# The first attention from tile 14 on: q and k come in as 32 by 32 blocks and VectorE transposes them, in place of TensorE

## The chip, the cores and the metric

One Trainium2 chip, of which the kernel uses one core. The metric is the device time of one execution in microseconds (us), the median of several executions; lower is better.

## The reference

Three layers follow one another, all in fp32. B = 8 sequences of S = 576 tokens, 8 heads of 64.

```python
# 1. attention inside chunks of 64 tokens (the "first attention")
scores = q_c @ k_c.T / sqrt(64)            # per batch, head, chunk: 64 x 64
attn = exp(scores - max); attn /= sum + 1e-9
x = (attn @ v_c)                           # heads side by side: B, S, 512
# 2. a mixing layer: each token with the one before it
xk = mu_k * x + (1 - mu_k) * x_prev;  xr = mu_r * x + (1 - mu_r) * x_prev
k = relu(xk @ w_k)                         # 512 -> 1024
v = (k * k) @ w_v                          # 1024 -> 512
r = sigmoid(xr @ w_r)                      # 512 -> 512
x = r * v
# 3. four experts, each a causal attention of one head of 64, the best two of four weighted
```

## The kernel before

`attn_mix` computes layers 1 and 2 together, `experts` layer 3 behind it. Nothing of `experts` is changed.

The 4608 tokens are cut in 36 tiles of 128 tokens, that is two chunks of 64, for the first attention, and in 12 units of 384 tokens for the mixing layer. For a tile the attention has these steps:

- `load_qk(t)` (L100): SP issues the loads of q and k of a tile. The buffers `ldq` and `ldk` are two deep, so the load of tile t + 2 is issued by `s_T(t)` when tile t has been read.
- `s_T(t)` (L132): `to_sbuf` turns q and then k by four TensorE transposes each (L127, into the PSUM bank `Tps`) and copies the result to SBUF by ScalarE (L129, `qT` and `kT`, two deep).
- `s_S(j)` (L142) takes a pair of tiles, 2j and 2j + 1: 64 matmuls of 64 x 64 on quarters of the TensorE array give the scores (`Sps`, L154). Then the softmax: VectorE takes the maximum (`m<-Sps`, L159) and subtracts it (`P<-Sps,m`, L160), ScalarE takes the exponential (L163), VectorE the sum (`m<-P`, L165) and its reciprocal (L167), GpSimd multiplies (L168).
- `s_PT(t)` turns the weights by four TensorE transposes (`Tps<-ident,P`), `s_PV(j)` (L172) multiplies by v (64 matmuls, L184) and ScalarE copies to `XT`. `load_v` (L107) loads v, which has four DMAs a tile.

The mixing layer of unit u has, in groups of 12 matmuls that each fill one of three PSUM buffers `mps`: 4 groups `mix_r` (emptied by ScalarE, L257), 8 groups `mix_k` and 4 double groups `mix_v`. A group of `mix_k` is emptied by ScalarE (L267, relu) and then VectorE (L270, `r<-mps,r`, which reads the PSUM buffer too and so sets it free); `kh` (ScalarE, L273) and `kl` (GpSimd, L274) are what `mix_v` reads. `mix_v` is emptied by VectorE (`x2o`, L289). The shifted inputs are made by GpSimd (`xa`, L228), VectorE (`xa`, L242; `xlr` and `xlk`, L244) and ScalarE (L243).

The steps of the attention are put between the groups of the mixing layer by a credit that is counted up with each group; the attention runs up to four units ahead of the mixing. The order on each engine is then fixed by a scheduler at build time, and each engine runs its list in order: an instruction that waits holds all that stand behind it on its engine. SP likewise issues its DMAs in the order of its list. The call `S` of pair j and `PV` of pair j - 1 stand together.

Of the kernel before, what the change touches and what calls it, by code (L numbers as in the profile page):

```python
# [8 lines left out]
F32 = mybir.dt.float32  # L9
# [10 lines left out]

CH = 64
UNIT = 384
CFG = dict(ps=(2, 3, 1, 2), P=5, sm=3, load=5, lag=(3, 4), out=(5, 1), qk1=(1, 1), qk0=(9, 1.1), v=(10, 0.9), order=((3, 0), (2, 0), (0, 0), (4, 0), (1, 0), (3, 1), (2, 1), (0, 1), (1, 1)), after=1, conv='v', clo='v', chi='g', x2hi='g', x2lo='v', ylo='g', yhi='v', xt='aa', r2='av', klo='vg', amul='vg', nearly=2, x2b=1, yb=4, qb=4, direct=((0, 1), (1, 1), (1, 1)), tailAV=4, kp=2, yt=1, yf=2, zb=1, om=(3, 2, 1, 0, 4), hp=1000, x2d=2, early=(2, 1), dact=3, rate0=0.43, rate=0.45, sh=(10, 12, 2), sh2=(11, 1, -1), pro='cccqqaacavvcaaaaacaacaaaascc', alag=2, seq=0, end=2, outL=(11, 2), outE=2, kcp='aa', dsc='v', ldb=2, vb=2, cn=512, stb=2, xb=4, pa=5, tb=2, first_j=7)
SEG = 192


# [7 lines left out]
def eng(nc, c):  # L34
    return nc.vector if c == "v" else nc.gpsimd
# [6 lines left out]
def copy(nc, c, out, in_):  # L42
    if c == "a":
        nc.scalar.activation(out=out, in_=in_, func=ACTF.Copy)
    else:
        eng(nc, c).tensor_copy(out, in_)
# [15 lines left out]
def attn_mix(tc, at, x2T, q, k, v, mu_k, mu_r, w_k, w_v, w_r, ident, attended_all, mixed_k):  # L62

    nc = tc.nc
    B, H, S, D = q.shape
    HP = H // 2
# [10 lines left out]
    with ExitStack() as ctx:  # L77
        wts = ctx.enter_context(tc.tile_pool(name="wts", bufs=1))
        mx = ctx.enter_context(tc.tile_pool(name="mx", bufs=1))
        ps = ctx.enter_context(tc.tile_pool(name="psM", bufs=1, space=PSUM))  # L80

        pa_open = ExitStack()
        pa = pa_open.enter_context(tc.tile_pool(name="psA", bufs=1, space=PSUM, side="right"))
# [9 lines left out]
        qkv = {}  # L93

        def runs(t):
            b, s = divmod(t * 128, S)
            return [(0, b, s, 128)] if s + 128 <= S else [(0, b, s, CH), (CH, b + 1, 0, CH)]

        def load_qk(t):
            for src, nm in ((q, "q"), (k, "k")):  # L100
                x = at.tile([128, H * D], F32, tag="ld" + nm, bufs=CFG["ldb"], name="ld" + nm)
                for p, b, s, n in runs(t):
                    nc.sync.dma_start(out=x[p:p + n].rearrange("p (h d) -> p h d", h=H),
                                      in_=src[b, :, s:s + n, :].rearrange("h p d -> p h d"))
                qkv[nm, t] = x

        def load_v(t):  # L107
            x = at.tile([128, 2, HP, D], F32, tag="ldv", bufs=CFG["vb"], name="ldv")
            for c in range(2):
                b, s = divmod(t * 128 + c * CH, S)  # L110
                for e in range(2):
                    r = e ^ c
                    nc.sync.dma_start(out=x[r * 64:(r + 1) * 64, c],
                                      in_=v[b, e::2, s:s + CH, :].rearrange("g p d -> p g d"))
            qkv["v", t] = x

        qT, kT, PP, PT, XT = {}, {}, {}, {}, {}
        nT = NU * TPU

        def bank(nm):  # L120
            return pa.tile([128, HP, 128], F32, tag="A", bufs=CFG["pa"], name=nm)

        def to_sbuf(src, nm):

            p = bank("Tps")
            for g in range(HP):
                nc.tensor.transpose(p[:, g], src[:, g * 128:(g + 1) * 128], ident)  # L127
            o = at.tile([128, HP, 128], F32, tag=nm, bufs=CFG["tb"], name=nm)
            nc.scalar.activation(out=o, in_=p, func=ACTF.Copy)  # L129
            return o  # L130

        def s_T(t):  # L132
            qT[t] = to_sbuf(qkv.pop(("q", t)), "qT")
            kT[t] = to_sbuf(qkv.pop(("k", t)), "kT")
            if t + CFG["ldb"] < nT:
                load_qk(t + CFG["ldb"])

# [6 lines left out]
        def s_S(j):  # L144
            banks = [bank("Sps").rearrange("p g (i k) -> p i g k", i=2) for _ in range(2)]
            for i in range(2):
                a, b = qT.pop(2 * j + i), kT.pop(2 * j + i)
                for g in range(HP):
                    for c in range(2):
                        for o in range(2):  # L150
                            e = o ^ c
                            r, cc = slice(e * 64, e * 64 + 64), slice(c * CH, (c + 1) * CH)
                            with tc.high_priority(1000) if j < CFG["first_j"] else nullcontext():
                                nc.tensor.matmul(out=banks[o][cc, i, g], lhsT=a[r, g, cc], rhs=b[r, g, cc],  # L154
                                                 start=True, stop=True)
            m = at.tile([128, 2, 2, HP], F32, tag="m", name="m")
            e = at.tile([128, 2, HP, 2, CH], F32, tag="P", name="P")
            for o, p in enumerate(banks):
                nc.vector.tensor_reduce(m[:, o], p, axis=AXX, op=ALU.max)  # L159
                nc.vector.tensor_tensor(e[:, :, :, o], p, m[:, o].unsqueeze(3).to_broadcast([128, 2, HP, CH]),  # L160
                                        op=ALU.subtract)
            ef = e.rearrange("p i g o k -> p (i g o) k")
            nc.scalar.activation(out=ef, in_=ef, func=ACTF.Exp, scale=scale)  # L163
            z = m.rearrange("p o i g -> p (o i g)")
            nc.vector.tensor_reduce(z, ef, axis=AXX, op=ALU.add)  # L165
            nc.vector.tensor_scalar(z, z, 1e-9, None, op0=ALU.add)
            nc.vector.reciprocal(z, z)  # L167
            eng(nc, CFG["amul"][j >= CFG["first_j"]]).tensor_tensor(  # L168
                ef, ef, z.unsqueeze(2).to_broadcast([128, 2 * H, CH]), op=ALU.mult)
            for i in range(2):  # L170
                PP[2 * j + i] = e[:, i]

        def s_PV(j):
            banks = [bank("PVps").rearrange("p g (i k) -> p i g k", i=2) for _ in range(2)]
            for i in range(2):
                t = 2 * j + i
                a, vt = PT.pop(t), qkv.pop(("v", t))
                for g in range(HP):
                    for c in range(2):
                        for o in range(2):  # L180
                            e = o ^ c
                            r, cc = slice(o * 64, o * 64 + 64), slice(c * CH, (c + 1) * CH)
                            with tc.high_priority(1000) if j < CFG["first_j"] else nullcontext():
                                nc.tensor.matmul(out=banks[c][e * 64:e * 64 + 64, i, g], lhsT=vt[r, c, g],  # L184
                                                 rhs=a[r, g, cc], start=True, stop=True)
            for c, p in enumerate(banks):

                done = 0
                while done < 2:
                    (u, k), n = divmod(4 * j + c + 2 * done, CH_U), 1  # L190
                    if u not in XT:
                        XT[u] = wkr.tile([128, HP, NSEG, SEG + 1], F32, tag="XT", bufs=CFG["xb"], name="XT")
                    sg, o = divmod(k, CPS)
                    if done == 0 and o + 2 < CPS:
                        n = 2
                    dst = XT[u][:, :, sg, 1:].rearrange("p g (w q) -> p w g q", q=CH)[:, o:o + 2 * n - 1:2]
                    copy(nc, CFG["xt"][u >= CFG["nearly"]], dst, p[:, done:done + n])
                    done += n
            for i in range(2):
                if 2 * j + i + CFG["vb"] < nT:  # L200
                    load_v(2 * j + i + CFG["vb"])
# [137 lines left out]
        for j in range(nT // 2 + 1):  # L339
            two = (2 * j, 2 * j + 1)  # L340
            attn += [(t // TPU, s_T, t) for t in two if t < nT]
            attn += [((t - 2) // TPU, s_PT, t - 2) for t in two if t > 1]
            attn.append(((2 * j - 1) // TPU if j else 0, s_SPV, j))
            attn += [(t // TPU, s_prev, t // TPU) for t in (2 * j - 2, 2 * j - 1) if t > 0 and t % TPU == TPU - 1]
# [32 lines left out]
        for c in CFG["pro"]:  # L377
            if c == "a":
                attend(2)
            elif c == "c":  # L380
                convert(1)
            elif c in loads:
                (load_qk if c == "q" else load_v)(next(loads[c]))
            else:
                attended(0)
                first_shift()

        credit = 0.0
        for u in range(NU):
# [6 lines left out]
            for i, (f, *args) in enumerate(items):  # L396
# [10 lines left out]
                if u + 1 < NU:  # L407
                    both = u + 1 <= CFG["sh2"][2]
                    for ws, at0 in (((1, 0), CFG["sh2"][0]),) if both else (((1,), CFG["sh"][0]), ((0,), CFG["sh"][1])):
                        g, r = divmod(i - at0, CFG["sh2" if both else "sh"][1 if both else 2])  # L410
# [508 lines left out]
```

## Time and profile before

| | |
|---|---|
| median of 3 runs (lowest to highest) | 1025.69 us (1022.12 to 1026.83) |
| the profiled execution | 1027.89 us |
| its span, from the first to the last instruction | 1026.1 us |
| granted TensorE clock over the span | 0.977 of full speed |
| busy over the span | PE 95%, PEld 91%, DVE 65%, ACT 56%, POOL 39% |
| from 183 to 510 us, where q and k of tiles 14 to 35 are turned | PE 324.8 of 327.0 us busy |

PE is TensorE's matmuls, PEld its weight loads, DVE VectorE, ACT ScalarE, POOL GpSimd, SP SyncE (SPq its DMA issues). The attention of all tiles ends at about 546 us; the experts take the rest. Busy shares are means over stages with different limits, so a change is judged in the stretch in which it stands.

### The profile page before, as it was taken

Reading aid. Unit: us, or ns where it says so; the run is one execution under the profiler, and the core shown is the slowest. Engines: PE = TensorE matmul, PEld = TensorE weight load, DVE = VectorE, ACT = ScalarE, POOL = GpSimd, SP = SyncE. Lnnn points to the kernel's source line nnn. Section 1 sums busy time; section 2 is a strip of 40 time slices with the busy share of each in tenths; the row PEclk is TensorE's granted clock in tenths of the full one; section 3 lists DMA queues with packets and bytes.
Section 4 is the critical chain, followed back from the end, with each engine's and each line's share of the span. In section 5 each row is a group of like instructions: output and inputs, shape, how many; then the busy total and the mean of one; then the engine's idle time right before and its main releaser. Section 6 shows DMA issues by size and latency. Waiting matters only on the chain.

```text
span 1026.1 us, 21849 instructions
## 1 busy us (share of the span) xinstructions
PE 972.5 (95%) x8214; PEld 934.0 (91%) x8214; DVE 664.5 (65%) x1646; ACT 570.0 (56%) x1315; POOL 395.6 (39%) x519
## 2 busy tenths in 40 slices
PE   3679899999999999999999999999999999999997
PEld 2569899998999999999999999989899999999986
DVE  5899935446544755565556541477776967787896
ACT  2478664545354636454635324266766757686675
POOL 5343312535453645364545443721341332133101
PEclk8588999999999999999999999999999999999999
DMA  8684432251324242425031211863545446262512
GB/s 220 176 210 134 113 84 73 52 124 43 98 48 124 63 104 48 114 45 126 22 83 39 76 47 37 190 160 86 172 96 160 136 117 183 68 178 69 171 42 95
DMA packets 170081, 108.39 MB, mean 106 GB/s; under 512 B 134024, under 2 KB 146424, under 8 KB 169976
## 3 DMA queue, kind: packets, MB, share of 16 engines
q1 hardware_dynamic: 139704, 67.14, 26.2%
q0 software_dynamic: 30272, 39.86, 14.3%
q8 instruction: 65, 1.06, 0.4%
q14 instruction: 40, 0.33, 0.1%
HBM read 66.01 MB, written 28.38 MB: 92 GB/s over the span
## 4 chain that ended last, share of the span: by engine, by line
PE 74%; DVE 12%; ACT 5%; DMA 4%; issue 2%; POOL 1%; SPq 1%; DVEq 0%; ACTq 0%; POOLq 0%
PE mps L57 14%; PE mps L59 14%; PE mps L58 14%; PE pj L57 6%; PE pj L59 5%; PE pj L58 5%; PE Sps L622 4%; PE Tps L127 3%; PE Tps L682 3%; PE AVps L715 2%; PE AVps L711 2%; PE Sps L154 2%; DVE PTl L689 1%; PE PVps L184 1%; DVE sm L624 1%
## 5 line engine op out<-in xcount | busy, mean ns | idle before, releaser
L57 PE MATMUL mps<-xhk,wkh 128*128 128x384 f32 x384 | 132.7, 347 | 2.0 <-DVE r L270 2.0
L58 PE MATMUL mps<-xlk,wkh 128*128 128x384 f32 x384 | 129.6, 338 | 0.0
L59 PE MATMUL mps<-xhk,wkl 128*128 128x384 f32 x384 | 129.4, 337 | 0.0
L57 PE MATMUL mps<-kh,wvh 128*128 128x384 f32 x384 | 129.1, 340 | 0.0
L58 PE MATMUL mps<-kl,wvh 128*128 128x384 f32 x384 | 127.7, 335 | 0.1
L59 PE MATMUL mps<-kh,wvl 128*128 128x384 f32 x384 | 126.9, 335 | 0.9 <-DVE wvl L325 0.9
L274 POOL TENSOR_TENSOR kl<-r,kh 128x384 fp32r<-128x384 f32 x80 | 86.1, 1080 | 79.7 <-ACT kh L273 79.5
L270 DVE TENSOR_TENSOR r<-mps,r 128x384 f32<-128x384 f32 x80 | 44.3, 554 | 99.8 <-ACT r L267 99.6
L634 ACT ACTIVATE P<-sm,nm 128x512 f32<-128x512 f32 (+3 forms) x144 | 83.9, 584 | 24.1 <-DVE nm L624 19.8
L228 POOL TENSOR_TENSOR xa<-XT 128x384 f32<-128x384 f32 x72 | 68.2, 955 | 62.3 <-DVE xlr L244 36.8
L624 DVE CUSTOM_DVE_ANT_0 sm<-Sps,mask 128x256 f32<-128x256 f32 (+4 forms) x160 | 74.2, 477 | 21.9 <-PE Sps L622 20.8
L731 POOL TENSOR_TENSOR Yf<-Yf,zb 128x576 f32<-128x576 f32 x14 | 20.0, 1430 | 153.5 <-DVE Yf L726 153.3
L57 PEld LDWEIGHTS mps<-xhk,wkh 128*128 128x128 f32 x384 | 72.9, 190 | 3.0 <-DVE r L270 2.5
L689 DVE TENSOR_TENSOR PTl<-Tps,PTh 128x512 fp32r<-128x512 f32 (+2 forms) x144 | 70.6, 504 | 7.0 <-ACT PTh L688 5.6
L242 DVE SCALAR_TENSOR_TENSOR xa<-xa,mu,XT 128x384 f32<-128x384 f32 x72 | 63.7, 900 | 15.0 <-POOL xa L228 14.9
L59 PEld LDWEIGHTS mps<-kh,wvl 128*128 128x128 f32 x384 | 71.8, 188 | 1.2 <-DVE wvl L325 1.2
L58 PEld LDWEIGHTS mps<-xlk,wkh 128*128 128x128 f32 x384 | 72.7, 189 | 0.1
L59 PEld LDWEIGHTS mps<-xhk,wkl 128*128 128x128 f32 x384 | 72.6, 189 | 0.0
L58 PEld LDWEIGHTS mps<-kl,wvh 128*128 128x128 f32 x384 | 72.1, 188 | 0.4 <-POOL kl L274 0.4
L57 PEld LDWEIGHTS mps<-kh,wvh 128*128 128x128 f32 x384 | 72.0, 188 | 0.4
L273 ACT ACTIVATE kh<-r 128x384 fp32r<-128x384 f32 x96 | 50.9, 530 | 37.9 <-DVE r L270 36.9
L57 PE MATMUL mps<-xhr,wrh 128*128 128x384 f32 x192 | 66.8, 350 | 4.5 <-ACT sig L257 3.3
(186 smaller groups left out, 2820.2 us busy)
## 6 DMA issues: line engine op xcount, KB each, us to landing
x2T<-x2d POOLq DMA_DIRECT2D x48, 384.0 KB, 3.1
x<-x2T POOLq DMA_DIRECT2D x32, 576.0 KB, 5.6
ldv<-in_v_dram SPq DMA_DIRECT2D x144, 64.0 KB
ldq<-in_q_dram SPq DMA_DIRECT2D x32, 256.0 KB
ldk<-in_k_dram SPq DMA_DIRECT2D x32, 256.0 KB
K<-Kph SPq DMA_DIRECT2D x64, 128.0 KB
out_dram<-o SPq DMA_DIRECT2D x32, 256.0 KB
st<-in_moe_w_k_dram SPq DMA_DIRECT2D x8, 512.0 KB
```

Of the source, the lines that this page charges most:

```text
L57: nc.tensor.matmul(out=out, lhsT=ah, rhs=bh, start=first and i == 0, stop=False)
L58: nc.tensor.matmul(out=out, lhsT=ah, rhs=bl, start=False, stop=False)
L59: nc.tensor.matmul(out=out, lhsT=al, rhs=bh, start=False, stop=last and i == n - 1)
L228: nc.gpsimd.tensor_tensor(d, now, prev, op=ALU.subtract)
L242: nc.vector.scalar_tensor_tensor(a, d, m, prev, op0=ALU.mult, op1=ALU.add)
L270: nc.vector.tensor_tensor(r2, p, r, op=ALU.mult)
L273: nc.scalar.activation(out=o.hi, in_=r2, func=ACTF.Copy)
L274: eng(nc, CFG["klo"][u >= CFG["nearly"]]).tensor_tensor(o.lo, r2, f32(o.hi), op=ALU.subtract)
L622: issued = nc.tensor.matmul(out=pp[:, :w], lhsT=x, rhs=y[:, a:a + w], start=n == 0, stop=n == len(terms) - 1)
L624: nc.vector.tensor_tensor_reduce(out=sm[:, a:a + w], in0=pp[:, :w], in1=mk[:, :w], op0=ALU.add, op1=ALU.min, scale=-scale, scalar=3e38, ac ...
L634: nc.scalar.activation(out=x[:, :nk], in_=sm[:, :nk], func=ACTF.Exp, scale=-1.0, bias=nm[:, :1], accum_out=z)
L689: nc.vector.tensor_tensor(l, src, f32(h), op=ALU.subtract)
```

## The change

The settings gain `dve_j=7`, and `by_dve(t)` holds for tiles 14 to 35. For these tiles:

- q and k are loaded by eight DMAs each, of 32 rows x 8 heads x 32 numbers (128 bytes in a piece, where there were 256), so that each 32 x 32 block lies in place for VectorE, whose transpose turns blocks of 32 x 32. There are 16 DMAs a tile, where there were two (four at a tile that lies across two sequences).
- One VectorE transpose of 128 x 512 each makes `qT` and `kT`. The eight TensorE transposes and two ScalarE copies of a tile are gone, and so are the two PSUM banks that they took.
- The halves of the 128 rows of `qT` and `kT` now hold the two chunks, where they held even and odd heads. The matmuls of `s_S` and `s_PV` are as many and as large; each half of the rows now writes one PSUM bank alone, where before both halves wrote both banks.
- v is loaded by one DMA a tile (two across sequences) where there were four.

```diff
+        def by_dve(t):
+            return t >= 2 * CFG["dve_j"]
+
         def load_qk(t):
             for src, nm in ((q, "q"), (k, "k")):
+                if by_dve(t):
+                    x = at.tile([128, H, 2, 32], F32, tag="ld" + nm, bufs=CFG["ldb"], name="ld" + nm)
+                    for c in range(2):
+                        b, s = divmod(t * 128 + c * CH, S)
+                        for i in range(2):
+                            for w in range(2):
+                                r = c * CH + i * 32
+                                nc.sync.dma_start(out=x[r:r + 32, :, w],
+                                                  in_=src[b, :, s + w * 32:s + w * 32 + 32, i * 32:i * 32 + 32]
+                                                  .rearrange("h p d -> p h d"))
+                    qkv[nm, t] = x.rearrange("p h w d -> p (h w d)")
+                    continue
...
         def load_v(t):
+            if by_dve(t):
+                x = at.tile([128, H, D], F32, tag="ldv", bufs=CFG["vb"], name="ldv")
+                for p, b, s, n in runs(t):
+                    nc.sync.dma_start(out=x[p:p + n], in_=v[b, :, s:s + n, :].rearrange("h p d -> p h d"))
+                qkv["v", t] = x
+                return
...
+        def by_blocks(src, nm):
+            o = at.tile([128, HP, 128], F32, tag=nm, bufs=CFG["tb"], name=nm)
+            nc.vector.transpose(o.rearrange("p g t -> p (g t)"), src)
+            return o.rearrange("p g (o t) -> p g o t", o=2)
+
         def s_T(t):
-            qT[t] = to_sbuf(qkv.pop(("q", t)), "qT")
-            kT[t] = to_sbuf(qkv.pop(("k", t)), "kT")
+            f = by_blocks if by_dve(t) else to_sbuf
+            qT[t] = f(qkv.pop(("q", t)), "qT")
+            kT[t] = f(qkv.pop(("k", t)), "kT")
...
+                                if by_dve(2 * j):
+                                    nc.tensor.matmul(out=banks[e][cc, i, g], lhsT=a[r, g, c], rhs=b[r, g, c],
+                                                     start=True, stop=True)
+                                    continue
...
+                                if by_dve(t):
+                                    nc.tensor.matmul(out=banks[o][cc, i, g], lhsT=vt[r, 2 * g + c],
+                                                     rhs=a[r, g, cc], start=True, stop=True)
+                                    continue
```

The order on the engines moves in three places. First TensorE, in a `mix_r` of the unit that runs at about 379 us (names carry buffer numbers; `mps_4552` and `mps_4584` before are `mps_4591` and `mps_4627` in the change). Before:

```order
L58 MATMUL mps_4552<-xlr_4243,wrh_89 128x384
L59 MATMUL mps_4552<-xhr_4242,wrl_90 128x384
L127 MATMUL Tps_4566<-ident_60,ldq_4176 128x128 x4
L127 MATMUL Tps_4573<-ident_60,ldk_4178 128x128 x4
L57 MATMUL mps_4584<-xhr_4242,wrh_89 128x384
L58 MATMUL mps_4584<-xlr_4243,wrh_89 128x384
```

and in the change:

```order
L58 MATMUL mps_4591<-xlr_4288,wrh_89 128x384
L59 MATMUL mps_4591<-xhr_4287,wrl_90 128x384
L57 MATMUL mps_4627<-xhr_4287,wrh_89 128x384
L58 MATMUL mps_4627<-xlr_4288,wrh_89 128x384
L59 MATMUL mps_4627<-xhr_4287,wrl_90 128x384
```

The two groups now follow one another. In the part of the list from the experts' first matmul on, TensorE's order is the same in both.

Second VectorE, at the softmax of the pair whose `S` runs at 336 us before, in the list between two evictions `r<-mps` of `mix_k` groups (`r_3976` and `r_4091` before are `r_4018` and `r_4128` in the change; lines are later by 28 to 35 there: L270 is L305, L159 is L190, L160 is L191, L165 is L196). Before:

```order
L270 TENSOR_TENSOR r_3976<-mps,r 128x384
L159 TENSOR_REDUCE m<-Sps 128x8 x2
L160 TENSOR_TENSOR P<-Sps,m 128x8x64 x2
L165 TENSOR_REDUCE m<-P 128x16
L270 TENSOR_TENSOR r_4091<-mps,r 128x384
```

and in the change, from behind `r_4018` on:

```order
L155 STREAM_TRANSPOSE qT<-ldq 128x512
L155 STREAM_TRANSPOSE kT<-ldk 128x512
L190 TENSOR_REDUCE m<-Sps 128x8 x2
L155 STREAM_TRANSPOSE qT<-ldq 128x512
L155 STREAM_TRANSPOSE kT<-ldk 128x512
L191 TENSOR_TENSOR P<-Sps,m 128x8x64 x2
L277 SCALAR_TENSOR_TENSOR xa<-xa,mu,XT 128x384
L196 TENSOR_REDUCE m<-P 128x16
L277 SCALAR_TENSOR_TENSOR xa<-xa,mu,XT 128x384
L279 TENSOR_TENSOR xlr<-xa,xhr 128x384
L197 TENSOR_SCALAR m<-m 128x16
L305 TENSOR_TENSOR r_4128<-mps,r 128x384
```

The four transposes of the next pair of tiles stand inside the softmax of this pair (they need the `qT` and `kT` buffers that this pair's `S` sets free), at each of the eleven pairs alike; here an `xa` pair and an `xlr` have moved ahead of the eviction too.

Third SP, which issues the loads, for one pair of tiles in the middle of the stretch. Before:

```order
L113 DMA ldv<-in_v_dram 64x4x64 x8
L103 DMA ldq<-in_q_dram 128x8x64
L103 DMA ldk<-in_k_dram 128x8x64
L103 DMA ldq<-in_q_dram 128x8x64
L103 DMA ldk<-in_k_dram 128x8x64
```

and in the change:

```order
L111 DMA ldq<-in_q_dram 32x8x32 x4
L126 DMA ldv<-in_v_dram 128x8x64
L111 DMA ldq<-in_q_dram 32x8x32 x2
L126 DMA ldv<-in_v_dram 128x8x64
L111 DMA ldq<-in_q_dram 32x8x32 x2
L111 DMA ldk<-in_k_dram 32x8x32 x8
L111 DMA ldq<-in_q_dram 32x8x32 x8
L111 DMA ldk<-in_k_dram 32x8x32 x8
```

Twelve issues for a pair have become 34, and the two loads of v, which wait for the `PV` that sets their buffers free, stand among the first loads of q.

## Rows read from the trace of the kernel before

**Rows 1.** The page: busy time of the engines, and PE in 40 slices.
```profile
PE 972.5 (95%) x8214; PEld 934.0 (91%) x8214; DVE 664.5 (65%) x1646; ACT 570.0 (56%) x1315; POOL 395.6 (39%) x519
...
PE   3679899999999999999999999999999999999997
```

**Rows 2.** The view by stretches: busy us (instructions), clock, DMA share, GB/s.
```profile
core 0: us, PE busy (x) PEld busy (x) DVE busy (x) ACT busy (x) POOL busy (x), PEclk, DMA share, GB/s
183.00:510.00 327.00, 324.83 (x3102) 318.99 (x3101) 181.01 (x281) 164.49 (x313) 161.97 (x180) 0.99 0.33 78
```

**Rows 3.** The waits of PE from 150 to 560 us: total, times, longest.
```profile
PE mps L57 <- DVE r L270: 2.0, 2, 1.9
```

**Rows 4.** The timeline of PE around a tile's transposes: start, us, instruction.
```profile
216.87 0.34 PE L59 MATMUL mps<-kh,wvl 128*128 128x384 f32 x1
217.04 0.60 PE L127 MATMUL Tps<-ident,ldq 128*128 128x128 f32 x4
217.48 0.60 PE L127 MATMUL Tps<-ident,ldk 128*128 128x128 f32 x4
...
218.09 0.34 PE L58 MATMUL mps<-kl,wvh 128*128 128x384 f32 x1
```

**Rows 5.** Tiles ldq and ldk, 183 to 510 us: min/median/max ns, first and last start.
```profile
L127 PE MATMUL Tps<-ident,ldq x88: 270/272/273, 183.0 to 506.6; 128*128 128x128 f32 x88
...
L127 PE MATMUL Tps<-ident,ldk x88: 271/273/417, 189.7 to 507.0; 128*128 128x128 f32 x88
```

**Rows 6.** The timeline of PE: S and PV of a pair, and what follows.
```profile
400.30 1.16 PE L154 MATMUL Sps<-kT,qT 64*64 64x64 f32 x64
...
402.34 0.45 PE L57 MATMUL mps<-xhk,wkh 128*128 128x384 f32 x1
```

**Rows 7.** Groups of DVE instructions by line: count, busy us, mean ns, idle before.
```profile
L313 DVE TENSOR_SCALAR cz<-cz 128x512 int32<-128x512 int32 x20 | 9.5, 477 | 13.9 <-POOL cz L312 13.9
...
L159 DVE TENSOR_REDUCE m<-Sps 128x8 f32<-128x512 f32 x36 | 23.1, 683 | 5.5 <-PE Sps L154 5.5
...
L165 DVE TENSOR_REDUCE m<-P 128x16 f32<-128x1024 f32 x18 | 21.9, 1218 | 16.4 <-ACT P L163 16.4
```

**Rows 8.** The timeline of DVE at the softmax of the pair at 336 us.
```profile
337.22 1.29 DVE L159 TENSOR_REDUCE m<-Sps 128x8 f32<-128x512 f32 x2
338.43 1.28 DVE L160 TENSOR_TENSOR P<-Sps,m 128x512 f32<-128x512 f32 x2
341.20 1.22 DVE L165 TENSOR_REDUCE m<-P 128x16 f32<-128x1024 f32 x1 [1.50 <-ACT P L163]
342.34 0.55 DVE L270 TENSOR_TENSOR r<-mps,r 128x384 f32<-128x384 f32 x1
...
343.08 0.61 DVE L242 SCALAR_TENSOR_TENSOR xa<-xa,mu,XT 128x384 f32<-128x384 f32 x1
...
351.69 0.70 DVE L244 TENSOR_TENSOR xlr<-xa,xhr 128x384 fp32r<-128x384 f32 x1
```

**Rows 9.** The timeline of ACT there: the exponential.
```profile
340.11 1.06 ACT L163 ACTIVATE P<-P 128x1024 f32<-128x1024 f32 x1
```

**Rows 10.** The timeline of PE there: three groups of mix_k, from PV to the next transposes.
```profile
338.05 0.44 PE L57 MATMUL mps<-xhk,wkh 128*128 128x384 f32 x1
...
344.40 0.49 PE L127 MATMUL Tps<-ident,ldq 128*128 128x128 f32 x3
```

**Rows 11.** The timelines of PE and DVE at the pair at 495 us.
```profile
495.85 1.15 PE L184 MATMUL PVps<-PT,ldv 64*64 64x64 f32 x63
...
496.14 1.28 DVE L159 TENSOR_REDUCE m<-Sps 128x8 f32<-128x512 f32 x2
```

**Rows 12.** SP: eight issues of v in a row, and issues by tile (min/median/max ns).
```profile
307.82 5.95 SPq L113 DMA_DIRECT2D ldv<-in_v_dram  x8
...
L113 SPq DMA_DIRECT2D ldv<-in_v_dram x144: 595/614/1652, 10.7 to 529.6; - x144
...
L103 SPq DMA_DIRECT2D ldq<-in_q_dram x22: 367/374/732, 189.9 to 478.7; - x22
```

**Rows 13.** DMA issues, 200 to 450 us: count, KB, median us to landing.
```profile
x2T<-x2d POOLq DMA_DIRECT2D x20, 384.0 KB, 3.4
```

More of the change, by code (lines that the diff above doesn't have):

```diff
@@ L22 @@
 UNIT = 384
-CFG = dict(ps=(2, 3, 1, 2), P=5, sm=3, load=5, lag=(3, 4), out=(5, 1), qk1=(1, 1), qk0=(9, 1.1), v=(10, 0.9), order=((3, 0), (2, 0), (0, 0), (4, 0), (1, 0), (3, 1), (2, 1), (0, 1), (1, 1)), after=1, conv='v', clo='v', chi='g', x2hi='g', x2lo='v', ylo='g', yhi='v', xt='aa', r2='av', klo='vg', amul='vg', nearly=2, x2b=1, yb=4, qb=4, direct=((0, 1), (1, 1), (1, 1)), tailAV=4, kp=2, yt=1, yf=2, zb=1, om=(3, 2, 1, 0, 4), hp=1000, x2d=2, early=(2, 1), dact=3, rate0=0.43, rate=0.45, sh=(10, 12, 2), sh2=(11, 1, -1), pro='cccqqaacavvcaaaaacaacaaaascc', alag=2, seq=0, end=2, outL=(11, 2), outE=2, kcp='aa', dsc='v', ldb=2, vb=2, cn=512, stb=2, xb=4, pa=5, tb=2, first_j=7)
+CFG = dict(ps=(2, 3, 1, 2), P=5, sm=3, load=5, lag=(3, 4), out=(5, 1), qk1=(1, 1), qk0=(9, 1.1), v=(10, 0.9), order=((3, 0), (2, 0), (0, 0), (4, 0), (1, 0), (3, 1), (2, 1), (0, 1), (1, 1)), after=1, conv='v', clo='v', chi='g', x2hi='g', x2lo='v', ylo='g', yhi='v', xt='aa', r2='av', klo='vg', amul='vg', nearly=2, x2b=1, yb=4, qb=4, direct=((0, 1), (1, 1), (1, 1)), tailAV=4, kp=2, yt=1, yf=2, zb=1, om=(3, 2, 1, 0, 4), hp=1000, x2d=2, early=(2, 1), dact=3, rate0=0.43, rate=0.45, sh=(10, 12, 2), sh2=(11, 1, -1), pro='cccqqaacavvcaaaaacaacaaaascc', alag=2, seq=0, end=2, outL=(11, 2), outE=2, kcp='aa', dsc='v', ldb=2, vb=2, cn=512, stb=2, xb=4, pa=5, tb=2, first_j=7, dve_j=7)
 SEG = 192
```

## The prediction

> **What bounds the kernel now.** I read the page first: TensorE (PE) is busy 95% of the span, and in the 40 slices it stands at nine tenths from the eighth slice on [rows 1]. So PE looks like the bound, but a busy PE may hide waits. The view by stretches, for the stretch in which the transposes go away (183 to 510 us), shows PE busy 324.8 of 327.0 us, VectorE 181.0, ScalarE 164.5, GpSimd 162.0, and the DMA engines busy a third of the time [rows 2]. The waits of PE from 150 to 560 us sum to 2.0 us, nearly all in one wait of 1.9 us for the eviction `r` on VectorE [rows 3]. So in this stretch time is PE's work and nothing else ends last: what is taken off PE comes off the end, as long as no other engine then makes PE wait. Behind the stretch PE's order is unchanged, so a shift passes on to the end.
>
> **What goes from PE.** Around one tile's transposes the timeline of PE has the last matmul before at 216.87 and the second behind at 218.09: 1.22 us [rows 4]. Two plain matmuls take 0.35 us: three groups, 36 matmuls, run from 338.05 to 344.40, which is 0.174 us each with 0.1 for the start [rows 10]. So eight transposes cost 0.87 us, the slower matmul behind them included. In the stretch there are 88 transposes of q and 88 of k [rows 5], 22 tiles of eight: 22 x 0.87 = **19.2 us less**. They all lie where PE has no idle time.
>
> The ScalarE copies of `qT` and `kT` go too. ScalarE is busy half the time [rows 2] and what it does is waited for only through VectorE; I take nothing for it. The PSUM banks that are set free are worth nothing either: no wait of PE for a bank of the attention is in its list [rows 3].
>
> **What comes to VectorE.** 44 transposes of 128 x 512. The trace has none. Nearest are passes over 512 columns: 477 ns for a simple operation from SBUF to SBUF, 683 ns for `m<-Sps`, and above them 1218 ns for a pass over 1024 [rows 7]. [...] The bounds for the range are 0.4 and 1.13 in a row, that is 477 and 1218 ns less the overlap of 0.08. VectorE has room for 44 x 0.6 = 26 us in sum. What counts is where they stand: all four of a pair lie in the middle of the softmax, ahead of the next eviction `r`, for which PE waits when its three buffers are full.
>
> I go through the places. At 336 us `m` started at 337.22, and an `r` at 342.34 [rows 8]. Now qT and kT go ahead of `m` and two more behind it: P ends at 337.22 + 2.4 + 1.21 + 1.28 = 342.1. The exponential (1.06 us [rows 9]), which had waited 0.4 us for its table, then ends at 343.2, the sum `m` (1.22) at 344.4, an `xa` and an `xlr` (0.61 and 0.70) at 345.7, a small operation (0.2), and `r` ends 0.55 later, at 346.5 [rows 8]. PE's three groups end at 344.4 [rows 10]. **PE waits 2.1 us** where it did not. The place at 238 us is alike (three groups behind `S`), and has the wait of 1.9 us already; I put 2.1 there. At 495 us the same sum from 496.14 gives `r` at 504.3 (no `xa` or `xlr` ahead, small operations of 0.4) against PV's end at 497.0 and 6.27 for three groups, 503.3 [rows 11]: 1.0 us. At 400 us `S` ends at 401.46, `r` by 409.2 and the copy `kh` by 409.8; PE reads it only after 47 matmuls in its new order, 402.34 + 8.2 = 410.5 [rows 6]: nothing. At the other seven places `S` stands in `mix_r`, which ScalarE empties, or in `mix_v`, whose double groups give 4.2 us a buffer: nothing. Sum 5.2, less the 2.0 that are there now: **3.2 us more**. With a transpose of 0.4 in a row it is about 1, with 1.13 about 11.
>
> [...]
>
> **What comes to SP and the DMA engines.** Each pair of tiles has 32 loads of q and k and two of v, where there were four and eight. An issue of a DMA holds SP: 0.37 us for 128 rows, 0.60 to 0.61 for 64 rows (1.65 once), and eight in a row take 5.95 us, 0.74 each with what lies between [rows 12]. For 32 rows there is no row; I take 0.74, since 64 rows are the nearest. The bounds are 0.37 and 1.65. A pair then needs 32 x 0.74 + 2 x 0.42 = 24.5 us of SP, and 3.4 us for the last to land (the nearest row is a store, [rows 13]): 27.9. A pair lasts (402.34 - 338.05) / 2 = 32.1 us now [rows 6, 10], less 1.75 = 30.4. The loads may start once the transposes of the pair before have read the buffers, and are needed one period later. So they come 2.5 us in time, and this costs nothing; the cover is gone above (30.4 - 4.2) / 32 = 0.82 us per issue. If one is late, the transposes wait, and behind them on VectorE the softmax and the evictions, for which PE waits. The DMA engines are no bound: even if all of their share of 0.33 [rows 2] were q and k, and a half piece took as long as a whole one, it would be 0.66.
>
> **The matmuls of S and PV.** 128 of them run from 400.30 to 402.34, 15.9 ns each [rows 6]. A transpose of 128 columns takes 109 ns, so 64 columns on a quarter of the array can't go below 13.6 ns a matmul: a gain of at most 0.29 us a pair, 3.2 in all, if the new division of rows and banks helps. If it halved the overlap, each pair would cost 2.04 us more, 22 in all. S and PV have different orders of the quarters now and the same pace, so I take nothing.
>
> [...]
>
> **Sum.** -19.2 + 3.2 = -16.0 us. Against the profiled execution, 1027.89, that is 1011.9. This execution lies 2.2 us (0.2%) above the median of the runs, 1025.69; against that, **1010 us**, 1.6% faster. 0.5%, 5 us, is about what a measurement of this kernel can tell from no change.
>
> **The rivals.**
> - *SP becomes the bound* (ends slower). Place: the loads of a pair, 32 issues in a row. Every 0.1 us per issue above 0.82 costs 3.2 us a pair, 35 in eleven pairs. From 0.86 on the gain is eaten; at 1.0 the time is about 1074 us. For it speaks that 64 rows cost more than 128, so that 32 may cost more again, and the one issue of 1.65; against it, that a load of v over 64 rows has 256 pieces, as many as a new load over 32 rows. Chance 0.13.
> - *VectorE takes most of it back*: transposes near the upper bound, or late by DMA waits. Four places then lose 2.1 us each more: 1018 us, up to 1022 with shift work (`xa`, `xlr`) late as well. Chance 0.18.
> - *No new wait at all and quicker S and PV*: -19.2 - 2.0 - 3.2 = -24.4, 1001 us. PE's waits above hang on a few tenths in each place. Chance 0.07.
> - *The quarters overlap less*: -16 + 22 = +6, 1032 us. Chance 0.04.
>
> **Chances.** The forecast (1004 to 1014 us) gets 0.58. Range **1003 to 1021**: it takes in the forecast and most of the VectorE rival, and leaves out SP, the overlap and most of the quickest case, about 2 in 10. Faster by over 0.5% (below 1020.6): 0.58 + 0.07 + 0.15 = 0.80. Within 0.5%: 0.07. Slower: 0.13.
>
> **What the changed profile would show.** Right: no `Tps<-ident,ldq` behind tile 13; the end of attention about 16 us earlier; PE's waits in the stretch some 5 us, for `r` on VectorE, at the pairs named; STREAM_TRANSPOSE near 0.65 us; issues of q and k 0.6 to 0.7 us each, with SP done before the next pair's `S`. Wrong: VectorE waiting for DMA ahead of `qT` or `kT`; issues above 0.8 us; transposes above 1 us; S and PV of a pair longer than 2.04 us; a pair's period above 32 us.

## The result and the profile after

The changed kernel took 1010.44 us (median of 4 runs, 1009.59 to 1011.45) against 1024.97 us (4 runs, 1022.12 to 1026.83): a ratio of 0.9861, interval 0.9834 to 0.9888, 14.5 us faster. The forecast was 1010.

The page after, busy time and PE in 40 slices, against [rows 1]; then the view by stretches, against [rows 2]:

```profile
PE 950.1 (94%) x8038; PEld 909.6 (90%) x8038; DVE 682.0 (68%) x1690; ACT 547.2 (54%) x1271; POOL 396.4 (39%) x519
...
PE   3679899998999999999999999999999999999997
```

```profile
183.00:510.00 327.00, 320.30 (x3127) 312.12 (x3126) 203.21 (x334) 143.16 (x271) 165.84 (x186) 1.00 0.40 83
```

176 PE instructions and 44 ScalarE copies are gone, 44 VectorE instructions came. PE is still the bound, but no longer without gaps: 6.7 of 327 us idle, against 2.2. Its waits from 165 to 510 us (line waited for, total, times, longest), against [rows 3]:

```profile
PE mps L57 <- DVE r L305: 5.2, 5, 1.5
PE mps L57 <- DVE x2o L324: 0.7, 1, 0.7
PE mps L57 <- ACT sig L292: 0.7, 2, 0.5
PE Tps L148 <- POOL P L199: 0.2, 1, 0.2
```

The spans of the two profiled executions (1026.1 and 1007.8 us) differ by 18.3 us, more than the medians. To see why, take two marks on PE's timeline, the `S` of the last pair turned by TensorE (pair 6) and of the last pair of all (pair 17). Before:

```profile
171.86 1.16 PE L154 MATMUL Sps<-kT,qT 64*64 64x64 f32 x64
...
522.68 1.16 PE L154 MATMUL Sps<-kT,qT 64*64 64x64 f32 x64
```

After:

```profile
167.90 1.16 PE L185 MATMUL Sps<-kT,qT 64*64 64x64 f32 x64
...
504.57 1.16 PE L182 MATMUL Sps<-kT,qT 64*64 64x64 f32 x64
```

Between the marks, 350.82 us became 336.67: **14.15 us less**. Behind the second mark both have 503 us left. The other 4.0 us lie ahead of the first mark, where PE's list is the same in both kernels. They are the spread of executions: a second profile of the changed kernel has its first mark at 169.85 us, and two runs below with the same PE list up to there have it at 172.10 (`e1_pe_kept`) and 169.36 us (`e2_half`, which is the kernel before up to tile 23). So this stretch between the marks, not the span, is compared below.

### The profile page after: what moved, and what is told of

It reads as the page before. It is cut to its first block, busy times and chain, and to the rows that moved or that the text cites. A ratio compares the mean times of both kernels' runs of the same rounds, so it can differ in the third digit from the quotient of the medians.

```text
span 1007.8 us, 21843 instructions
## 1 busy us (share of the span) xinstructions
PE 950.1 (94%) x8038; PEld 909.6 (90%) x8038; DVE 682.0 (68%) x1690; ACT 547.2 (54%) x1271; POOL 396.4 (39%) x519
## 3 DMA queue, kind: packets, MB, share of 16 engines
q0 software_dynamic: 30272, 39.86, 14.5%
## 4 chain that ended last, share of the span: by engine, by line
PE 53%; DVE 7%; ACT 2%; DMA 2%; issue 1%; POOL 0%; DVEq 0%; SPq 0%; ACTq 0%; POOLq 0%
PE mps L57 8%; PE mps L58 8%; PE mps L59 8%; PE pj L57 6%; PE pj L59 6%; PE pj L58 6%; PE Sps L657 4%; PE Tps L717 3%; PE AVps L750 2%; PE AVps L746 2%; DVE PTl L724 1%; DVE sm L659 1%; DMA x<-x2T 1%; ACT P L669 1%; DVE Q L554 1%
## 5 line engine op out<-in xcount | busy, mean ns | idle before, releaser
L305 DVE TENSOR_TENSOR r<-mps,r 128x384 f32<-128x384 f32 x80 | 44.4, 555 | 95.0 <-ACT r L302 83.3
```

Of the source, the lines that this page charges most:

```text
L305: nc.vector.tensor_tensor(r2, p, r, op=ALU.mult)
```

## The experiments

The kernel before ran beside each set of runs and took 1023.7 to 1025.0 us (medians) there, so times of different sets are compared to about 1 us.

**Which part pays.**

```diff
             nc.vector.transpose(o.rearrange("p g t -> p (g t)"), src)
+            p = bank("Tps")
+            for g in range(HP):
+                nc.tensor.transpose(p[:, g], src[:, g * 128:(g + 1) * 128], ident)
```

> The changed kernel, with the eight TensorE transposes of each tile from 14 on kept as extra work whose result is not read (the kernel still takes qT and kT from VectorE). Theory (the gain is TensorE's time for 22 x 8 transposes, 0.87 us a tile): 19 us come back, 1010.4 + 19 = 1028 to 1031 us, PE busy about 19 us more. Rival (the gain comes from what else goes: ScalarE's copies, their PSUM reads, the new division of rows and banks): it stays at 1009 to 1013.

Measured 1027.93 us (1026.79 to 1029.70), before 1024.63: ratio 1.0031 (1.0018 to 1.0043). With the transposes back on PE the time rises by 17.5 us, more than the 14.5 gained: the gain is PE's time, and the rest of the change has a price, 3.3 us above the kernel before. The prediction's sum had -19.2 and +3.2 for these two; the medians give -17.5 and +3.3. The split is not a clean one: between the marks this run takes 352.61 us, 15.9 more than the changed kernel, but its waits of PE sum to 4.3 us there where the changed kernel has 6.7. So by rows the work that was put back is some 18 us.

```diff
-dve_j=7
+dve_j=12
```

> dve_j=12: only tiles 24 to 35 are turned by VectorE. Theory (0.87 us a tile less on TensorE, and PE waits for VectorE only where four transposes stand in a softmax): 12 x 0.87 = 10.4 less, waits of 1.4 + 0.3 + 0.9 + 0.2 from 330 us on more, so 7.8 below the kernel before: 1016 to 1018 us. Rival (the gain is made at one end of the stretch, as by the loads or the early clock): near 1010 or near 1025.

Measured 1018.68 us (0.9941, 0.9922 to 0.9959): 6 us below the kernel before. The gain grows with the number of tiles, so the rival is out; it is 1.8 us short of the 7.8 expected. The last section has the likely reason.

**What a VectorE transpose costs where it stands.**

```diff
             nc.vector.transpose(o.rearrange("p g t -> p (g t)"), src)
+            nc.vector.transpose(o.rearrange("p g t -> p (g t)"), src)
```

> Each VectorE transpose is done twice. VectorE gets 44 x 0.6 = 26 us of work more, 2.4 us inside each softmax. Theory (PE waits for the eviction r behind the transposes; places with little slack): the five places with waits now lose 2 to 2.4 us more each, the others up to 1: 8 to 16 us more, 1018 to 1026 us, PE waits of 15 to 22 us in the stretch. Rival (PE's waits of 5 us come from something else, and VectorE, busy two thirds of the time, has room): 1009 to 1012.

Measured 1021.52 us (1017.98 to 1022.56), 11.1 above the changed kernel. The time is inside the theory's range, but PE's waits between the marks sum to 10.7 us, not 15 to 22. The timeline of PE at the longest wait, and the view by stretches there (the third figure from the right, 0.50, is the granted clock), show what else it costs:

```profile
341.93 0.69 PE L57 MATMUL mps<-xhk,wkh 128*128 128x384 f32 x1 [3.02 <-DVE r L306]
342.41 0.52 PE L58 MATMUL mps<-xlk,wkh 128*128 128x384 f32 x1
342.73 0.52 PE L59 MATMUL mps<-xhk,wkl 128*128 128x384 f32 x1
```

```profile
342.40:345.20 2.80, 2.80 (x10) 2.80 (x10) 2.80 (x3) 0.41 (x2) 2.80 (x2) 0.50 0.43 67
```

Behind a wait of 3.02 us the matmuls start 0.32 us apart instead of 0.174, about ten in a row: 1.5 us more, at half the clock. The same follows this run's waits of 2.61 and 1.82 us. So 4.0 us more of waits and three such stretches make 8.5 us; between the marks this run is 9.7 us longer than the changed kernel, and the rest is not accounted for. The profile is of the slowest of its executions (1022.56 us).

**Moving the transposes out of the softmax.** An order edge holds them back; `behind[j]` is the reciprocal of pair j's softmax:

```diff
+            with tc.issue_after(behind[t // 2 - 1].ins) if by_dve(t) else nullcontext():
                 qT[t] = f(qkv.pop(("q", t)), "qT")
                 kT[t] = f(qkv.pop(("k", t)), "kT")
```

> The four transposes of a pair are ordered behind the reciprocal of the softmax before them, so they no longer stand between S and its exponential, nor ahead of the next eviction r. Theory (PE's waits of 6.8 us in the stretch are these four transposes in the softmax): waits fall to about 2, as before the change, and the time by 4 to 6: 1004 to 1007 us. Rival (the waits are VectorE's sum of work, wherever it stands, or the loads come late once their buffers are freed 6 us later): no change, 1009 to 1012, or slower.

Measured 1008.73 us (1008.57 to 1011.46; ratio 0.9853, 0.9831 to 0.9874). PE's waits fell to 3.9 us, by less than expected, and the stretch between the marks to 335.55 us. Two waits stand close together at 331 and 333 us, and in this execution half a clock behind them takes 1.3 to 1.5 us back (its rows are in the last section):

```profile
331.58 0.66 PE L148 MATMUL Tps<-ident,P 128*128 128x128 f32 x4 [0.80 <-POOL P L202]
333.23 0.69 PE L57 MATMUL mps<-xhk,wkh 128*128 128x384 f32 x1 [0.99 <-DVE r L308]
```

Three more runs followed together: one that holds the transposes in program order, the changed kernel again, and this one again.

```diff
-            nc.vector.transpose(o.rearrange("p g t -> p (g t)"), src)
+            tc.keep_in_program_order(nc.vector.transpose(o.rearrange("p g t -> p (g t)"), src))
```

> The transposes of each tile are held at the place in VectorE's list where the program issues them: two behind the softmax, the other two some groups later, so that never more than 1.2 us of them stand in a row. Theory (PE waits where transposes stand ahead of an eviction for longer than its slack): PE's waits in the stretch fall to 1 or 2 us, 1004 to 1008 us. Rival (two transposes later, so loads start later: the buffers are freed up to 12 us after S, SP needs some 18 us a pair of 30): VectorE waits for DMA ahead of a qT, 1010 us or more.

> The changed kernel again, beside the two with moved transposes on one chip: 1009 to 1011.5 us by all theories.

> The transposes behind the softmax again, to tell 1008.7 from 1010.4 us: theory (2.9 us of waits less in the stretch, less what S in more pieces costs) 1.5 to 3 us below the changed kernel of the same job; rival (the order is worth nothing) within 1 us of it.

Measured: in program order 1012.72 us (1011.97 to 1013.75), the changed kernel again 1010.66 (1010.57 to 1010.75), behind the softmax again 1009.25 (1008.01 to 1013.37; ratio 0.986, 0.9838 to 0.9881). So transposes behind the softmax come out 1.7 us below the first runs of the changed kernel and 1.4 us below it when run beside it, and shorter between the marks (335.55 and 334.68 us against 336.67 and 336.20), but the runs overlap, and the difference is not established; 1.4 us lies between what its theory and its rival said.

Program order lost 2 us, but not by the rival: VectorE waits for no DMA there. At PE's longest wait (2.87 us, `r` at 337.73) no transpose stands ahead of `r` at all. The timelines of VectorE and of GpSimd there:

```profile
333.49 0.25 DVE L198 RECIPROCAL m<-m 128x16 f32<-128x16 f32 x1
333.66 1.49 DVE L277 SCALAR_TENSOR_TENSOR xa<-xa,mu,XT 128x384 f32<-128x384 f32 x2
335.22 2.58 DVE L279 TENSOR_TENSOR xlr<-xa,xhr 128x384 fp32r<-128x384 f32 x2
337.73 0.54 DVE L305 TENSOR_TENSOR r<-mps,r 128x384 f32<-128x384 f32 x1
```

```profile
334.64 2.28 POOL L199 TENSOR_TENSOR P<-P,m 128x1024 f32<-128x1024 f32 x1
```

The reciprocal releases GpSimd's multiply of the weights, and two `xlr`, 0.56 us each elsewhere, take 2.58 us: they end 0.88 us after the multiply does. The rows of all fourteen traces, between the marks, bear this out: the 14 `xlr` that start beside the multiply (at least 0.3 us before its end) take 1.2 to 2.3 us (median 2.11) where those beside an idle GpSimd take 0.56, and the 120 transposes that start beside it take 0.66 to 0.71, no longer than the others. No run moved the multiply by itself, so this reading rests on the rows. One more run held back only the second tile's two transposes (condition `by_dve(t) and t % 2`):

> Of each pair's four transposes, two stay ahead of the softmax and two are ordered behind its reciprocal. In the traces so far every single wait of PE of 1.8 us or more, and 0.8 + 1.0 us close together, is followed by some 3 us at half the granted clock, which costs about 1.5 us more; the changed kernel (1.48 + 1.07) shows none. Theory (what counts is the length of PE's single waits at the two places near 240 and 334 us): two transposes less ahead of r shorten them to about 0.8 and no stretch falls to half clock: 1007 to 1009 us. Rival (shift work moves up into the gap and r is no earlier, as in the run in program order): waits of 2 us and more with half clock behind them, 1010 to 1013.

Measured 1016.46 us (1014.79 to 1017.59; ratio 0.992, 0.990 to 0.994). What the rival said happened: two waits of 3.4 and 3.3 us for `r`, each with half the clock behind it; the time is 3.5 us above its range. The expectation read too much into the traces so far, though: in three of them PE's clock did not fall behind such waits (last section). VectorE and GpSimd at the second wait:

```profile
337.36 0.67 DVE L157 STREAM_TRANSPOSE kT<-ldk 128x512 f32<-128x512 f32 x1
337.95 2.05 DVE L280 SCALAR_TENSOR_TENSOR xa<-xa,mu,XT 128x384 f32<-128x384 f32 x2
339.92 0.54 DVE L308 TENSOR_TENSOR r<-mps,r 128x384 f32<-128x384 f32 x1
```

```profile
337.16 1.90 POOL L202 TENSOR_TENSOR P<-P,m 128x1024 f32<-128x1024 f32 x1
```

A transpose keeps its 0.67 us beside the multiply; the `xa` behind it, 0.6 us each where GpSimd is idle, last until the multiply's end and longer. With all four transposes behind the reciprocal they cover the multiply (329.62 to 331.52 us there, transposes until 331.67), which fits that run being the better one.

**The price of an issue on SP.**

```diff
-  nc.sync.dma_start(out=x[r:r + 32, :, w], in_=src[b, :, ...])
+  for h in (slice(0, HP), slice(HP, H)):
+      nc.sync.dma_start(out=x[r:r + 32, h, w], in_=src[b, h, ...])
```

> Each 32-row load of q and k is issued as two, of four heads each: 64 issues a pair where there were 32, the same bytes and pieces. In the changed kernel eight issues take 3.9 to 5.4 us, 0.49 each. Theory (an issue costs SP much the same whatever its number of pieces): 64 x 0.45 to 0.49 + 0.8 = 30 to 32 us of SP a pair and some 3 us to land, against a pair of 29 to 30 us: the loads come 3 to 6 us late each pair, VectorE waits for DMA ahead of qT, and the time is 1035 to 1075 us. Rival (an issue costs by its pieces, so half a load costs half): SP stays below 20 us a pair and the time at 1009 to 1013.

Measured 1053.87 us (1052.70 to 1054.71; ratio 1.0283). The theory holds. SP's rows for one pair, 16 issues each, and VectorE's largest sum of waits for a DMA:

```profile
263.54 8.56 SPq L112 DMA_DIRECT2D ldq<-in_q_dram  x16
272.19 8.92 SPq L112 DMA_DIRECT2D ldk<-in_k_dram  x16
...
282.31 8.41 SPq L112 DMA_DIRECT2D ldq<-in_q_dram  x16
290.82 8.34 SPq L112 DMA_DIRECT2D ldk<-in_k_dram  x16
```

```profile
DVE kT L156 <- DMA ldk<-in_k_dram: 33.5, 9, 7.1
```

Half a load costs as much SP time as a whole one (0.53 us against 0.54 below). SP is busy from 263.54 to 299.16 us for one pair, and the eleven pairs between the marks now last 380.93 / 11 = 34.6 us each instead of 30.6: SP has become the bound. Its issues follow one another without a gap from 225 to 345 us, and the DMA engines' busy share between the marks is 0.36, below the 0.40 of the changed kernel, so they are not what holds the loads up.

**The division of the PSUM banks.**

```diff
...
-  nc.tensor.matmul(out=banks[e][cc, i, g], lhsT=a[r, g, c], rhs=b[r, g, c], ...)      # S
+  nc.tensor.matmul(out=banks[o][cc, i, g], lhsT=a[r, g, c], rhs=b[r, g, c], ...)
...
-  nc.tensor.matmul(out=banks[o][cc, i, g], lhsT=vt[r, 2 * g + c], rhs=a[r, g, cc], ...)   # PV
+  nc.tensor.matmul(out=banks[e][cc, i, g], lhsT=vt[r, c, g], rhs=a[r, g, cc], ...)
```

> The division of the PSUM banks as before the change: in S and PV both halves of the rows write both banks again (v comes in the swapped order with four DMAs a tile); all else as changed. Theory (the division of banks is worth nothing: S and PV of a pair took 2.04 us in the kernel before and 2.03 in the changed one): no change, 1009 to 1012 us, and S to PV still 0.98 us. [...]

Measured 1010.15 us (1008.92 to 1010.89). PE's timeline in this run:

```profile
265.74 1.16 PE L186 MATMUL Sps<-kT,qT 64*64 64x64 f32 x64
266.73 1.11 PE L220 MATMUL PVps<-PT,ldv 64*64 64x64 f32 x64
```

S to PV takes 0.99 us, against 0.98 in the kernel before and the changed one: the division is worth nothing. Where the halves of the rows share a bank here, they write different partitions of it; a kernel in which they write the same ones was not tried.

**More tiles.** Both on top of the transposes behind the softmax:

```diff
-dve_j=7
+dve_j=6      # and 5 in the second run
```

> As the run with the transposes behind the softmax (1008.7 us), and tiles 12 and 13 turned by VectorE too (dve_j=6). Theory (TensorE bounds from about 120 us on, 0.87 us a tile): 1.7 us less, 1006 to 1008. Rival (VectorE, busy 57 of 60 us before 120 us, still bounds there, so what goes from TensorE is lost): 1008 to 1012.

> As before with dve_j=5: tiles 10 to 13 too. Theory: 3.5 us less than 1008.7, 1004 to 1007. Rival (VectorE bounds until about 120 us, where the transposes of tiles 10 and 11 fall): 1008 to 1014.

Measured 1014.87 us (1010.65 to 1017.49) and 1026.04 (1023.52 to 1029.34): nothing was gained, as the rivals said, but the times lie above their ranges too. The trace of the first run is of its quickest execution, 1010.65 us; the other five took 1014.56 to 1017.49, so where its 6 us went is not shown. The view by stretches of the second run, where PE sits idle 6 of 30 us and the clock falls to 0.74:

```profile
60.00:120.00 60.00, 47.31 (x574) 43.91 (x575) 57.27 (x100) 46.73 (x94) 21.91 (x20) 0.96 0.61 136
120.00:150.00 30.00, 23.79 (x294) 21.32 (x294) 19.49 (x32) 8.05 (x14) 7.40 (x14) 0.74 0.61 128
```

VectorE is full from 60 to 120 us, at 57 of 60 us, the conversion of the weights among its work; in the kernel before it is as full there, at 56.8. PE's largest sum of waits up to 250 us is 5.5 us, for VectorE's multiply of the attention weights. This fits the rival: the transposes must start where VectorE has room.

## Why the prediction was right

**What goes from PE: right, but some came back.** Forecast 19.2 us. The reading of [rows 4] holds at every tile whose eight transposes stand together in the kernel before: 0.87 to 0.88 us each. `e1_pe_kept` gives 17.5 by its medians and some 18 by its rows. In all, between the marks 14.15 us went although waits grew by 4.7 us (6.7 less 2.0), so 18.8 came off the rest of PE's time. That is not all transposes: about 1.5 us of it is a stretch at half the clock that the kernel before has and the changed kernel has not (below). So, as the remainder, other steps of PE grew by some 1.9 us, a term that the prediction did not have. The rows show where most of it lies: the changed kernel takes up the plain matmuls again behind transposes of the weights 30 times where the kernel before did so 23 times, and behind a wait 8 times instead of 2, and each such first matmul takes 0.26 to 0.28 us instead of 0.174; the plain matmuls in a row are slower by 0.8 us in all.

**The price of a transpose: right.** The tiles' rows (min/median/max ns), and VectorE's timeline at the pair at 231 us, which answers to [rows 8]:

```profile
L155 DVE STREAM_TRANSPOSE qT<-ldq x22: 683/699/712, 168.7 to 481.0; 128x512 f32<-128x512 f32 x22
...
L155 DVE STREAM_TRANSPOSE kT<-ldk x22: 662/669/712, 169.3 to 481.7; 128x512 f32<-128x512 f32 x22
```

```profile
232.28 0.70 DVE L155 STREAM_TRANSPOSE qT<-ldq 128x512 f32<-128x512 f32 x1
232.90 0.67 DVE L155 STREAM_TRANSPOSE kT<-ldk 128x512 f32<-128x512 f32 x1
233.50 1.25 DVE L190 TENSOR_REDUCE m<-Sps 128x8 f32<-128x512 f32 x2
234.67 0.69 DVE L155 STREAM_TRANSPOSE qT<-ldq 128x512 f32<-128x512 f32 x1
235.28 0.67 DVE L155 STREAM_TRANSPOSE kT<-ldk 128x512 f32<-128x512 f32 x1
...
240.46 0.55 DVE L305 TENSOR_TENSOR r<-mps,r 128x384 f32<-128x384 f32 x1
```

In a row they start 0.62 and 0.60 us apart; 0.60 was forecast. No row of the kernel before shows that term: it was the author's estimate, half of the 1.21 us that two `m<-Sps` of the same width take in a row in [rows 8], 0.08 us less than the 0.683 of one alone. The rows here show 0.62 and 0.60 for the transposes, and for the two `m<-Sps` between them 1.17 us to the next start.

**PE's waits: the sum right, the reason only in part.** The waits for `r` came where named, and sum to the 5.2 us forecast. PE's timeline at the first of each place:

```profile
241.06 0.44 PE L57 MATMUL mps<-xhk,wkh 128*128 128x384 f32 x1 [1.48 <-DVE r L305]
...
334.47 0.44 PE L57 MATMUL mps<-xhk,wkh 128*128 128x384 f32 x1 [1.42 <-DVE r L305]
...
486.81 0.44 PE L57 MATMUL mps<-kh,wvh 128*128 128x384 f32 x1 [0.85 <-DVE r L305]
```

They are 1.48 and then 1.07 behind the pair at 231 us (forecast 2.1), 1.42 and 0.34 at 324 (2.1), 0.85 at 477 (1.0). Another 1.6 us, for `x2o`, `sig` and `P`, stand at places that were put at nothing. So by rows the waits cost 4.7 us more, where the forecast had 3.2. Against that, the kernel before lost about 1.5 us to the half clock behind its wait of 1.9 (12 steps of PE took 3.39 us where they take 1.9 at full clock), which the prediction did not see; the changed kernel has no such stretch. The whole sum by rows is then -19.2 + 4.7 + 1.9 - 1.5 = -14.1 us, against -16.0 forecast: 1.5 us more of waits and the 1.9 us were not in it, and the 1.5 us of half clock, not foreseen either, made up for some of that, which is luck. That the time came within half a us of 1010 also owes 0.7 us to the kernel before, whose median is 1024.97 us here and was 1025.69 when the forecast was made; that too is luck.

The step said that four transposes push `r` back. They do: at 324 us, where the multiply starts behind `r` in both kernels, a wait of 1.42 us is new. But it matters as much whether GpSimd's multiply starts ahead of `r`. Before, at the wait of [rows 3], the rows of VectorE and GpSimd were:

```profile
246.76 2.19 DVE L244 TENSOR_TENSOR xlr<-xa,xhr 128x384 fp32r<-128x384 f32 x1
248.88 0.55 DVE L270 TENSOR_TENSOR r<-mps,r 128x384 f32<-128x384 f32 x1
```

```profile
246.41 2.13 POOL L168 TENSOR_TENSOR P<-P,m 128x1024 f32<-128x1024 f32 x1 [0.66 <-DVE m L167]
```

One `xlr` took 2.19 us beside the multiply. In the changed kernel the reciprocal (240.93) is behind `r` (240.46 above), the multiply starts only at 241.33, and the long instruction beside it, an `xa` of 2.25 us, delays the second `r` instead (1.07 us of wait). So at this place the transposes added 2.4 us to the softmax, and about as much went behind `r`: the first wait even fell, from 1.89 to 1.48 us. That the forecast of these places came out near the rows is partly luck: its sum had 0.70 us for an `xlr`, and the one beside the multiply took 2.19 where the 28 of the stretch have a median of 0.56.

**SP: nothing, as forecast, with a smaller issue.** SP's rows for one pair:

```profile
207.96 4.19 SPq L111 DMA_DIRECT2D ldq<-in_q_dram  x8
212.24 5.37 SPq L111 DMA_DIRECT2D ldk<-in_k_dram  x8
217.71 3.98 SPq L111 DMA_DIRECT2D ldq<-in_q_dram  x8
221.79 3.87 SPq L111 DMA_DIRECT2D ldk<-in_k_dram  x8
```

32 issues take 17.4 us, 0.54 each, where 0.74 was taken from the loads of v. The rival is real, as `e5_sp_twice` shows, but its price was too high: 64 issues of 0.53 us are 34 us a pair, 8 us above the 26.2 (32 x 0.82) that the prediction allowed, and cost 4.0 us a pair. The buffers come free tile by tile and SP goes on while loads land, so nearly the whole period is SP's to use.

**S and PV, ScalarE, DMA engines: nothing, as forecast.** The division of the PSUM banks has no effect on the time here, by the run with the banks shared (1010.15 against 1010.44 us). The floor of 13.6 ns a matmul was the author's estimate and no run shows it: S to PV, 64 matmuls, takes 0.98 us in both kernels, 15.3 ns each, and 0.99 us with the banks shared. ScalarE lost 21 us of work in the stretch and gave nothing back: `e1_pe_kept` is without its copies and no faster than the kernel before. The DMA share rose from 0.33 to 0.40, below the bound of 0.66.

## What to carry to other kernels

Work taken off an engine that was busy without gaps came off the time, here 14.5 us of 19.2, where the engine that took it over had room at that place, not only on average: the same move two tiles earlier cost 6 us, though where is not shown, and four tiles earlier, where VectorE is busy 57.27 of 60 us, 17 us. What the move cost was decided by all that stood ahead of the next eviction in VectorE's list (a new wait of 1.42 us at 324 us) and by what ran on GpSimd beside it (an `xlr` of 2.19 us against 0.56): with the transposes held in program order, two `xlr` of 2.58 us together came in, and the wait was 2.87 us. Each half of a load cut in two cost SP as much as a whole load, 0.53 us against 0.54; compare the issues of a period with the period, as here 34 us for 64 issues with a pair's 30.6.

## What was not expected of the hardware

Some waits of PE cost more than their length, by 1.3 to 1.5 us (below). The view by stretches behind the wait of 1.9 us in the kernel before, and then behind the wait of 1.42 us in the changed one:

```profile
251.00:254.20 3.20, 3.20 (x12) 3.10 (x12) 3.04 (x4) 2.66 (x7) 2.74 (x3) 0.50 0.00 0
```

```profile
334.50:337.00 2.50, 2.32 (x12) 2.00 (x12) 2.50 (x3) 0.85 (x2) 2.50 (x3) 1.00 0.44 68
```

The granted clock fell to 0.50 for some 3 us or longer behind each of ten single waits of PE between the marks (1.82 to 3.41 us, in the kernel before and four others), and stayed at 1.00 behind 1.42 and 1.68 us. But the length of the wait alone does not tell. In the two profiles of the kernel with the transposes behind the softmax, the same two waits stand close together (0.80 and 0.99 us, 0.81 and 0.99 us), and the clock fell in the first and not in the second, nor at the three such places in the runs with more tiles; and in the run with tiles 12 and 13 it stayed at 1.00 behind a single wait of 1.83 us. The stretches behind the two pairs of waits, and then that wait and the stretch behind it:

```profile
333.20:336.60 3.40, 3.37 (x11) 3.38 (x12) 3.24 (x5) 2.29 (x6) 2.89 (x3) 0.51 0.41 64
```

```profile
333.80:337.20 3.40, 3.40 (x19) 3.40 (x20) 3.24 (x5) 2.27 (x6) 2.91 (x3) 1.00 0.46 71
```

```profile
147.24 0.44 PE L57 MATMUL mps<-xhk,wkh 128*128 128x384 f32 x1 [1.83 <-ACT r L305]
```

```profile
147.20:150.60 3.40, 3.36 (x19) 3.36 (x20) 2.13 (x5) 3.34 (x8) 0.00 (x0) 1.00 0.45 69
```

What decides it besides the length is not shown by these runs. The two profiles of the one kernel also give the price: between the marks the first is 0.9 us longer although its waits are 0.4 us shorter, so its stretch at half the clock cost 1.3 us. By the spacing of matmuls (0.32 us apart instead of 0.174) it is about 1.5, and no list of waits shows it. The profiled execution of `e2_half` has two such stretches (behind 1.89 and 2.49 us), that of the kernel before one and that of the changed kernel none; one more would account for most of the 1.8 us that `e2_half` is short, which is likely and not tested.
